# Local and global attention, then a gated feed-forward: four word and four merged buffers for the weight conversion, and the short product of the global queries issued first

## The chip, the cores and the metric

The kernel runs on one core of a Trainium2 chip. A core has five engines that run their own instruction queues and meet at semaphores: TensorE (matrix products; PE in the profile, with its weight loads as PEld), VectorE (DVE), ScalarE (ACT), GpSimd (POOL) and SyncE (SP), which here only issues transfers. The metric is the time of one execution on the device, in microseconds (us); lower is better.

## The reference: what is computed

Eight batches of eight heads, 512 local positions with 64 dimensions, and 32 global tokens. A local query sees the local keys within 32 positions and all global keys; a global query sees all keys. The attention output, 4608 rows of 512, goes through a gated feed-forward layer of width 1536.

```python
k_all, v_all = concat(k_g, k_l), concat(v_g, v_l)
out_g = softmax(q_g @ k_all.T / 8) @ v_all
s_ll  = where(abs(i - j) <= 32, q_l @ k_l.T / 8, -1e9)
out_l = softmax(concat(q_l @ k_g.T / 8, s_ll)) @ concat(v_g, v_l)
x     = concat(out_g, out_l) as rows of 8 heads * 64
y     = (sigmoid(x @ w_gate) * (x @ w_val)) @ w_out
```

The three weight matrices reach the device as 64-bit floating-point numbers: `w_gate` and `w_val` 512 x 1536, `w_out` 1536 x 512.

## The kernel before

**Precision by two terms.** A float32 operand is split into a rounded part (`hi`) and the remainder (`lo`), both of a type that TensorE takes in one pass; a product is then three products, hi*hi, lo*hi and hi*lo. Where a tile is called native (`nat`), float32 is multiplied as it is, without a split. That is so in the first two chunks and in the first four heads of the third.

**Chunks.** The rows are worked in chunks: two of 256 rows for batch 0, then one of 512 rows for each other batch, and at the end one of 256 rows that holds the global tokens of all batches. For each chunk `ffn_stream` yields the products of the feed-forward layer piece by piece: for each of 12 blocks of the inner width (`f`), twelve products for the gate (`bank_g`, L380), twelve for the value (`bank_v`, L380), then those with `w_out` (`bank_o`, L414). The attention of a later chunk runs between them.

**An order by due times.** `att_events` gives each step of the attention a due time, counted in pieces of the feed-forward stream; L496 to L518 put these steps and the weight conversion into one list, sort it by time and order number, and L520 to L526 run the steps as the stream reaches their times. Steps due at or before zero run ahead of the stream. What the code issues is then laid out, engine by engine, by the scheduler of the programming layer, which also gives out the slots of the tile pools and sets the semaphores.

**Attention units.** A head of a full chunk has two local units (`local_unit`) and one global unit (`global_unit`). A local unit: scores into `bank_x` (L237), mask and row minimum on VectorE (L251), exponential on ScalarE (L254), scaling (L223 or L225), transposes through TensorE into `bank_y` (L268), a copy to `pt` (L276 native; else L279 for the rounded part and L280 for the remainder), products with the values (L290 and L291 native, L298 and L299 split). A global unit: the 32 global queries of the head, `qg`, against all keys. The four windows of local keys go in two halves into `sa`, a `bank_x` tile of 32 x 512 (L317); the 32 global keys go into `sb`, a `bank_y` tile of 32 x 32 (L319). Each needs two products in the split case, so that the unit has four with 256 columns and two with 32, all with `qg` as the stationary operand. Then the maxima of both (L322, L323), the exponentials (L326, L327), scaling, transposes (L335) and the products with the values (L348). All of `bank_x`, `bank_y`, `bank_g` and `bank_v` share four banks of PSUM (tag `att`). In the units of the first chunk TensorE also runs `fill`, small products whose result nothing uses (L113).

**Weight conversion.** The weights are fetched as words, two 32-bit words a number, in 36 pieces: for each `f`, 128 columns of `w_gate`, the same of `w_val`, and 128 rows of `w_out` (`w_src`). `stage(i)` has SP load piece i, 512 KB, into a word buffer (L129). `convert(i, hi, lo)` builds float32 from the words in a merged buffer: the sign (L140), the high word rescaled on VectorE or ScalarE by turns (L146 or L144), the low word's bits (L147), the high word's bits (L148); ScalarE rounds that into `hi` (L149), GpSimd subtracts for `lo` (L150). At its end it calls `stage` for the next piece that takes the same word buffer. Pieces 0 to 2 are tied by `issue_after` to the last L251 issued at that point; later pieces are not. The converted `w_gate` and `w_val` stay in SBUF; `w_out` goes to device memory (L161, L162) and is fetched again for each use (L405).

**Buffers.** One tile of the pool `xp`, `words`, of 4096 words a partition, holds three word buffers of 1024 and two merged buffers of 512 (L476 to L478). Piece i takes buffer i modulo their number. The pool has two slots; the other holds `xts[0]`, the input of the feed-forward layer for the first two chunks. L513 starts the loads of the first three pieces at the time -1002. The operands `q` and `k` of the first chunk's heads are loaded at -1016 (heads 0 and 1), -1008 (2 and 3), -1000 (4 and 5) and -992 (6 and 7), the values at -1004 and -988.

Of the kernel before, what the change touches and what calls it, by code (L numbers as in the profile page):

```python
# [10 lines left out]
U32 = mybir.dt.uint32  # L11
# [6 lines left out]
P = 128  # L18
# [38 lines left out]
def kernel(ctx, tc, qk, v, w_gate, w_val, w_out, out_l, out_g):  # L57
    nc = tc.nc
# [4 lines left out]
    const = ctx.enter_context(tc.tile_pool(name="const", bufs=1))  # L63
# [52 lines left out]
    conv_bufs = []  # L116
# [8 lines left out]
    def stage(i):  # L125
        if i < len(w_src):
            src = w_src[i]
            st = conv_bufs[0][i % len(conv_bufs[0])].rearrange("p (t n) -> p t n", t=src.shape[1])
            nc.sync.dma_start(st, src)  # L129
# [91 lines left out]
    def scaled(kind, out, in_, by):  # L221
        if NORM[kind][cnt["norm"] % len(NORM[kind])] == "s":
            nc.scalar.mul(out, in_, by)  # L223
        else:
            nc.vector.tensor_scalar(out, in_, by, None, op0=ALU.mult)  # L225
        cnt["norm"] += 1
# [78 lines left out]
    def global_unit(T, b, h):  # L305
        ks, k0s, q0 = T["qk"], T["k0"], T["q0"]
        nat = T["native"]
        last = len(ks) - 1
        prow, kt = 64 * (h % 2), h // 2
        qg = ks[0][:, QK - SG - q0:QK - q0]  # L310
        sa = ps.tile([32, 4, P], F32, name="bank_x", tag="att", bufs=4)
        sb = ps.tile([32, 32], F32, name="bank_y", tag="att", bufs=4)
        for half in range(2):
            o0 = 96 * half
            for t, (src, k0) in enumerate(zip(ks, k0s)):
                view = src[:, k0 + 32:k0 + 32 + 4 * BLK].rearrange("p (j c) -> p j c", c=BLK)[:, :, o0:o0 + 64]
                nc.tensor.matmul(sa[:, :, 64 * half:64 * half + 64], qg, view, start=t == 0, stop=t == last)  # L317
        for t, (src, k0) in enumerate(zip(ks, k0s)):
            nc.tensor.matmul(sb, qg, src[:, k0 + 96:k0 + 128], start=t == 0, stop=t == last)  # L319
        mg = small.tile([32, 4], F32, name="mg")  # L320
        saf = sa.rearrange("p a c -> p (a c)")
        nc.vector.tensor_reduce(mg[:, 0:1], saf, axis=AX.X, op=ALU.max)  # L322
        nc.vector.tensor_reduce(mg[:, 1:2], sb, axis=AX.X, op=ALU.max)  # L323
        nc.vector.tensor_scalar(mg[:, 2:3], mg[:, 0:1], mg[:, 1:2], -0.125, op0=ALU.max, op1=ALU.mult)
        sg = small.tile([32, 2], F32, name="sg")
        nc.scalar.activation(pg[:, 0:512], saf, AF.Exp, bias=mg[:, 2:3], scale=0.125, accum_out=sg[:, 0:1])  # L326
        nc.scalar.activation(pg[:, 544:576], sb, AF.Exp, bias=mg[:, 2:3], scale=0.125, accum_out=sg[:, 1:2])  # L327
        yield
        nc.vector.tensor_scalar(mg[:, 3:4], sg[:, 0:1], sg[:, 1:2], 1e-9, op0=ALU.add, op1=ALU.add)
        nc.vector.reciprocal(mg[:, 3:4], mg[:, 3:4])  # L330
        scaled(0, pg[:, 0:576], pg[:, 0:576], mg[:, 3:4])
        yield
        pt_ps = ps.tile([P, 5, 32], F32, name="bank_y", tag="att", bufs=4)
        for j in range(5):
            nc.tensor.transpose(pt_ps[:, j], pg[:, j * P:(j + 1) * P], ident[0:32, 0:32])  # L335
        if nat:
            pt = att.tile([P, 5, 32], F32, name="ptg_nat", tag="ptg", bufs=1)
            nc.scalar.copy(pt, pt_ps)
        else:
            pt = att.tile([P, 5, 64], F32R, name="ptg", bufs=1)  # L340
            nc.scalar.copy(pt[:, :, 0:32], pt_ps)
            nc.vector.tensor_tensor(pt[:, :, 32:64], pt_ps, pt[:, :, 0:32].bitcast(F32), op=ALU.subtract)
        yield
        vt = T["v"]
        xg = xg32[prow:prow + 64, kt, b * SG:(b + 1) * SG]
        o_ps = ps.tile([64, 32] if nat else [P, 64], F32, name="bank_x", tag="att", bufs=4)
        for j in range(5):
            nc.tensor.matmul(o_ps, vt[:, (VM + VS)[j], :], pt[:, j, :], start=j == 0, stop=j == 4)  # L348
        if nat:
            nc.scalar.copy(xg, o_ps)  # L350
            return
        y = att.tile([64, 64], F32, name="y", bufs=1)
        nc.scalar.copy(y, o_ps[64:128])
        nc.vector.tensor_tensor(y, o_ps[0:64], y, op=ALU.add)
        nc.gpsimd.tensor_tensor(xg, y[:, 0:32], y[:, 32:64], op=ALU.add)
# [118 lines left out]
    xts = {0: xp.tile([P, 2, KT, 512], F32R, name="xt")}  # L474
    xts[1] = xts[0]
    words = xp.tile([P, 4096], U32, name="xt")  # L476
    conv_bufs.append([words[:, i * 1024:(i + 1) * 1024] for i in range(3)])
    conv_bufs.append([words[:, 3072 + i * 512:3072 + (i + 1) * 512] for i in range(2)])  # L478

    chs = []  # L480
    for ci, (b, blocks, _) in enumerate(chunks):
# [14 lines left out]
    queue = att_events(0, -1000, START["per0"]) + att_events(1, START["base1"], START["per1"])  # L496
# [10 lines left out]
    for f in range(NF):  # L507
# [2 lines left out]
        queue.append((g, 4, lambda f=f: convert_w(f, 0)))  # L510
        queue.append((v_, 4, lambda f=f: convert_w(f, 1)))
        queue.append((o, 4, lambda f=f: convert_wo(f)))
    queue.append((-1002, 2, lambda: [stage(i) for i in range(3)]))  # L513

    def split_globals():
        for kt in range(KT):
# [65 lines left out]
```

## Time and profile before

| | us |
|---|---|
| three runs, median | 1262.37 |
| their lowest and highest | 1262.34, 1264.86 |
| the profiled execution | 1262.67 |
| its span, first to last instruction | 1260.8 |
| ScalarE: L254 busy | 113.8 |
| GpSimd: L401 busy | 137.6 |
| VectorE: L225 into `p_buf` busy | 151.8 |

How to read the lines further down: a group of instructions gives line, engine, operation, tiles (out<-in), shapes and count; after the bar the busy time and the mean duration of one in ns; after the second bar the engine's idle time just before them, and what ended it. A line of the timeline gives the start and the duration in us, then engine, line and operation; a count above one means merged neighbours, and the bracket at its end tells the idle time before it and the releaser. A stretch gives for each engine the busy time and, in brackets, the number of instructions.

### The profile page before, as it was taken

How to read it: one execution, taken by the hardware profiler on the slowest of the kernel's cores; microseconds unless marked ns; L12 is line 12 of the kernel's file. 1: busy time of each engine (PE TensorE's matmuls, PEld its weight loads, DVE VectorE, ACT ScalarE, POOL GpSimd, SP SyncE). 2: the span in 40 equal slices, each digit the busy share in tenths (PEclk: the TensorE clock that was granted, in tenths of full speed). 3: DMA queues.
4: the chain of work that ended last, by engine and by line, in shares of the span. 5: the costliest groups of instructions: out<-in, count | busy, mean ns of one | idle time of the engine just before them, and what ended most of it. 6: DMA issues, size and time to landing. Idle time of an engine off the chain costs nothing.

```text
span 1260.8 us, 20601 instructions
## 1 busy us (share of the span) xinstructions
PE 1223.5 (97%) x6884; PEld 998.6 (79%) x6884; DVE 878.9 (70%) x2433; ACT 782.9 (62%) x1899; POOL 571.1 (45%) x573
## 2 busy tenths in 40 slices
PE   8899989999999999999999999999999999999998
PEld 6677768788778877888788877888788877888897
DVE  6888977757876778758776778767875787632232
ACT  5686766756666666656765766656665666532333
POOL 2444545535555455545554455535554545311111
PEclk9798999999999999999999999999999999999999
DMA  6686754333333333333334333333333332122243
GB/s 232 215 264 219 255 172 125 107 97 108 92 103 113 113 92 108 109 106 112 100 86 120 121 100 100 108 112 109 91 107 114 108 92 88 51 84 67 67 134 117
DMA packets 59497, 151.90 MB, mean 120 GB/s; under 512 B 6144, under 2 KB 19456, under 8 KB 59392
## 3 DMA queue, kind: packets, MB, share of 16 engines
q1 hardware_dynamic: 59392, 150.59, 39.3%
q8 instruction: 54, 0.88, 0.3%
q14 instruction: 51, 0.42, 0.1%
HBM read 135.36 MB, written 15.20 MB: 119 GB/s over the span
## 4 chain that ended last, share of the span: by engine, by line
PE 73%; DVE 16%; ACT 6%; issue 4%; DMA 1%; POOL 0%; POOLq 0%; DVEq 0%; ACTq 0%; SPq 0%
PE bank_g L380 19%; PE bank_v L380 18%; PE bank_o L414 18%; PE bank_x L237 4%; PE bank_y L268 4%; DVE p_buf L225 3%; DVE th L396 2%; PE bank_y L335 2%; PE bank_x L348 2%; DVE pg_buf L225 2%; PE bank_x L298 2%; ACT s_sb L254 1%; PE bank_x L299 1%; PE bank_x L317 1%; DVE pt L280 1%
## 5 line engine op out<-in xcount | busy, mean ns | idle before, releaser
L380 PE MATMUL bank_g<-xt,wg 128*128 128x512 f32 (+1 forms) x1440 | 340.2, 371 | 1.8 <-DVE th L398 1.8
L380 PE MATMUL bank_v<-xt,wv 128*128 128x512 f32 (+1 forms) x1440 | 332.7, 368 | 3.0 <-DVE pt L280 2.7
L414 PE MATMUL bank_o<-wo,hh 128*128 128x512 f32 x1224 | 334.1, 404 | 0.8 <-ACT hh L400 0.4
L380 PEld LDWEIGHTS bank_g<-xt,wg 128*128 128x128 f32 x1440 | 238.6, 191 | 41.7 <-issue 3.5
L380 PEld LDWEIGHTS bank_v<-xt,wv 128*128 128x128 f32 x1440 | 237.8, 190 | 40.7 <-PE bank_y L319 3.1
L414 PEld LDWEIGHTS bank_o<-wo,hh 128*128 128x128 f32 x1224 | 214.1, 189 | 38.9 <-ACT hh L400 1.2
L401 POOL TENSOR_TENSOR hh<-th,hh 128x512 fp32r<-128x512 f32 (+1 forms) x120 | 137.6, 1147 | 200.7 <-ACT hh L400 199.8
L254 ACT ACTIVATE s_sb<-s_sb,nm 128x224 f32<-128x224 f32 x240 | 113.8, 475 | 142.9 <-DVE nm L251 141.8
L225 DVE TENSOR_SCALAR p_buf<-s_sb,r 128x128 f32<-128x128 f32 (+1 forms) x443 | 151.8, 386 | 4.2 <-PE bank_y L268 0.4
L393 DVE TENSOR_SCALAR mn<-bank_g 128x512 f32<-128x512 f32 (+1 forms) x108 | 67.3, 623 | 110.8 <-ACT th L388 109.4
L396 DVE SCALAR_TENSOR_TENSOR th<-th,mn 128x512 f32<-128x512 f32 (+1 forms) x120 | 102.0, 850 | 59.9 <-ACT mn L394 53.6
L206 POOL TENSOR_TENSOR kl<-qk_raw,qk_hi 128x704 fp32r<-128x704 f32 x52 | 88.4, 1700 | 116.0 <-ACT qk_hi L205 116.0
L303 POOL TENSOR_TENSOR x<-t 64x256 f32<-64x256 f32 x104 | 76.1, 732 | 142.7 <-DVE t L302 138.5
L388 ACT ACTIVATE th<-bank_g 128x512 f32<-128x512 f32 (+1 forms) x120 | 63.5, 530 | 98.0 <-PE bank_g L380 96.5
L400 ACT CAST hh<-th 128x512 fp32r<-128x512 f32 (+1 forms) x120 | 66.5, 554 | 68.6 <-DVE th L398 68.1
L251 DVE CUSTOM_DVE_ANT_0 s_sb<-bank_x,masks 128x224 f32<-128x224 f32 x240 | 83.8, 381 | 12.6 <-PE bank_x L237 8.2
L208 POOL TENSOR_TENSOR qk_hi<-qk_raw,qk_hi 64x256 fp32r<-64x256 f32 x104 | 87.8, 863 | 4.1
L268 PE MATMUL bank_y<-ident,p_buf 128*128 128x128 f32 x496 | 78.7, 279 | 9.4 <-DVE p_buf L225 5.1
L268 PEld LDWEIGHTS bank_y<-ident,p_buf 128*128 128x128 f32 x496 | 60.3, 142 | 29.5 <-ACT pg_buf L326 6.6
L257 DVE TENSOR_SCALAR r<-sm 128x2 f32<-128x2 f32 x128 | 29.3, 229 | 75.8 <-ACT s_sb L254 74.1
L205 ACT CAST qk_hi<-qk_raw 128x1248 fp32r<-128x1248 f32 x52 | 64.1, 1233 | 22.3 <-PE bank_y L319 22.2
L398 DVE TENSOR_TENSOR th<-bank_v,th 128x512 f32<-128x512 f32 (+1 forms) x120 | 72.4, 603 | 5.0 <-PE bank_v L380 1.3
(111 smaller groups left out, 1994.6 us busy)
## 6 DMA issues: line engine op xcount, KB each, us to landing
wo<-wo_dram SPq DMA_DIRECT2D x116, 512.0 KB, 3.5
qk_raw<-in_qk_dram SPq DMA_DIRECT2D x104, 312.0 KB, 4.5
v_raw<-in_v_dram SPq DMA_DIRECT2D x52, 256.0 KB, 2.6
out_dram<-ob SPq DMA_DIRECT2D x34, 256.0 KB, 2.9
xt<-in_w_gate_dram SPq DMA_DIRECT2D x12, 512.0 KB, 4.7
xt<-in_w_val_dram SPq DMA_DIRECT2D x12, 512.0 KB, 4.1
xt<-in_w_out_dram SPq DMA_DIRECT2D x12, 512.0 KB, 4.9
v_nat<-in_v_dram SPq DMA_DIRECT2D x8, 512.0 KB, 4.5
```

What stands on the lines that cost most here:

```text
L206: nc.gpsimd.tensor_tensor(kl, t[:, K0:Q1], hi[:, K0:Q1].bitcast(F32), op=ALU.subtract)
L208: nc.gpsimd.tensor_tensor(hi[64:128, r], t[64:128, r], hi[64:128, r].bitcast(F32), op=ALU.subtract)
L225: nc.vector.tensor_scalar(out, in_, by, None, op0=ALU.mult)
L251: anchor[0] = nc.vector.tensor_tensor_reduce(out=s_sb[:, i], in0=s_ps[:, i, 0:WIN], in1=masks[:, m], scale=-0.125, scalar=3.0e38, op0=ALU. ...
L254: nc.scalar.activation(s_sb[:, i], s_sb[:, i], AF.Exp, bias=nm[:, i:i + 1], scale=-1.0, accum_out=sm[:, i:i + 1])
L268: nc.tensor.transpose(pt_ps[:, 2 * i + t], pb[:, i, t * P:(t + 1) * P], ident)
L303: nc.gpsimd.tensor_tensor(dst, t0[:, :, 0], t0[:, :, 1], op=ALU.add)
L380: nc.tensor.matmul(acc, w[a][:, t, fs], xt[:, c, t, x0:x0 + ntok], start=n == 0, stop=n == 11)
L396: nc.vector.scalar_tensor_tensor(th, th, 1.0, mn, op0=ALU.add, op1=ALU.mult)
L398: nc.vector.tensor_tensor(th, acc, th, op=ALU.mult)
L401: nc.gpsimd.tensor_tensor(hh[:, 1, 0:ntok], th, hh[:, 0, 0:ntok].bitcast(F32), op=ALU.subtract)
L414: nc.tensor.matmul(o_ps[t], ph[:, a, t * P:(t + 1) * P], pwo[:, c], start=f2 == 0 and i == 0, stop=f2 == NF - 1 and i == 2)
```

## The change

1. In `global_unit` the two products into `sb` are issued ahead of the four into `sa`. The tiles are still allocated in the same order.
2. A new tile `more` of 2048 words a partition gives a fourth word buffer and, together with the end of `words`, four merged buffers in place of two.
3. The loads of four pieces, not three, are started at the time -1002. `convert` takes the number of buffers from the lists, so that it now stages the piece four further on.
4. The scratch for DMA descriptors in SBUF is set to 1024.

```diff
         sb = ps.tile([32, 32], F32, name="bank_y", tag="att", bufs=4)
+        for t, (src, k0) in enumerate(zip(ks, k0s)):
+            nc.tensor.matmul(sb, qg, src[:, k0 + 96:k0 + 128], start=t == 0, stop=t == last)
         for half in range(2):
...
                 nc.tensor.matmul(sa[:, :, 64 * half:64 * half + 64], qg, view, start=t == 0, stop=t == last)
-        for t, (src, k0) in enumerate(zip(ks, k0s)):
-            nc.tensor.matmul(sb, qg, src[:, k0 + 96:k0 + 128], start=t == 0, stop=t == last)
...
-    conv_bufs.append([words[:, i * 1024:(i + 1) * 1024] for i in range(3)])
-    conv_bufs.append([words[:, 3072 + i * 512:3072 + (i + 1) * 512] for i in range(2)])
+    more = const.tile([P, 2048], U32, name="words_more")
+    room = [words[:, i * 512:(i + 1) * 512] for i in range(8)] + [more[:, i * 512:(i + 1) * 512] for i in range(2048 // 512)]
+    conv_bufs.append([words[:, i * 1024:(i + 1) * 1024] for i in range(3)] + [more[:, i * 1024:(i + 1) * 1024] for i in range(1)])
+    conv_bufs.append((room[6:8] + room[8 + 2 * 1:])[0:4])
...
-    queue.append((-1002, 2, lambda: [stage(i) for i in range(3)]))
+    queue.append((-1002, 2, lambda: [stage(i) for i in range(4)]))
...
-    nc = bacc.Bacc("TRN2", target_bir_lowering=False, num_devices=1)
+    nc = bacc.Bacc("TRN2", target_bir_lowering=False, num_devices=1, dynamic_dma_scratch_size=1024)
```

## The prediction

> **What bounds the kernel now.** The page first: the totals, the strip of forty slices, the chain that ended last.
>
> ```profile
> span 1260.8 us, 20601 instructions
> PE 1223.5 (97%) x6884; PEld 998.6 (79%) x6884; DVE 878.9 (70%) x2433; ACT 782.9 (62%) x1899; POOL 571.1 (45%) x573
> ...
> PEclk9798999999999999999999999999999999999999
> ...
> PE 73%; DVE 16%; ACT 6%; issue 4%; DMA 1%; POOL 0%; POOLq 0%; DVEq 0%; ACTq 0%; SPq 0%
> ```
>
> TensorE is busy 97% of the span and carries 73% of the chain; VectorE is next with 16%. The strip says where to look closer: the granted clock falls below full only in the first slices. The view by stretches splits the span (columns: PE, PEld, DVE, ACT, POOL busy, then clock, DMA share, GB/s).
>
> ```profile
> 4.00:12.00 8.00, 8.00 (x52) 7.24 (x53) 3.76 (x20) 1.97 (x8) 0.00 (x0) 1.00 1.03 361
> 36.00:50.00 14.00, 12.65 (x49) 10.06 (x50) 8.74 (x26) 7.44 (x18) 5.96 (x5) 0.53 0.72 238
> 97.00:100.40 3.40, 2.19 (x18) 1.51 (x17) 3.40 (x9) 1.58 (x5) 1.62 (x2) 1.00 0.82 284
> 100.40:107.20 6.80, 6.80 (x24) 4.83 (x25) 5.66 (x18) 3.57 (x13) 0.55 (x1) 0.50 0.69 241
> 110.70:114.10 3.40, 3.40 (x17) 3.18 (x16) 2.75 (x8) 2.42 (x7) 0.29 (x1) 0.50 0.14 52
> 115.00:172.00 57.00, 50.32 (x330) 39.16 (x329) 55.22 (x126) 39.15 (x111) 29.76 (x23) 1.00 0.77 245
> 172.10:175.50 3.40, 3.40 (x17) 3.40 (x17) 1.42 (x7) 2.87 (x10) 2.33 (x3) 0.50 0.28 101
> 260.00:360.00 100.00, 99.08 (x546) 80.99 (x545) 74.32 (x209) 63.85 (x153) 47.51 (x49) 1.00 0.34 104
> ```
>
> There are two regimes. From about 220 us on TensorE sets the pace (99.08 of 100 us busy). Before about 175 us the weights are converted between the attention units, and the pace changes hands: VectorE holds it from 115 to 172 (55.22 of 57 us), TensorE at about half clock from 36 to 50 and in three shorter stretches. The first part of the change acts in both regimes, the buffers in the early one only.
>
> **Part 1: the short product first.** A global unit issues four long products (L317, 256 columns) and two short ones (L319, 32 columns). One unit from the timeline (columns: start, duration, engine, line):
>
> ```profile
> 328.12 0.18 PE L319 MATMUL bank_y<-kl,qk_hi 128*32 128x32 f32 x1
> 328.16 1.19 PE L414 MATMUL bank_o<-wo,hh 128*128 128x512 f32 x4
> ...
> 329.87 0.36 PE L298 MATMUL bank_x<-pt,vhl 128*128 128x256 f32 x1 [0.52 <-DVE pt L280]
> ...
> 330.30 0.28 PE L299 MATMUL bank_x<-pt,vhl 128*128 128x256 f32 x1
> 330.42 1.09 PE L414 MATMUL bank_o<-wo,hh 128*128 128x512 f32 x4
> ```
>
> Four products of L414 take 1.19 us behind the short product and 1.09 us behind a 256-column one. I read the 0.10 us as a weight load that the short product is too short to cover. The load rows give a second measure:
>
> ```profile
> L299 PEld LDWEIGHTS bank_x<-pt,vhl 128*128 128x128 f32 x208 | 39.2, 188 | 2.4
> L317 PEld LDWEIGHTS bank_x<-kl,qk_hi 128*32 128x32 f32 x104 | 11.2, 108 | 6.7
> L319 PE MATMUL bank_y<-kl,qk_hi 128*32 128x32 f32 x52 | 9.5, 183 | 0.0
> L319 PE MATMUL bank_y<-qk_nat 64*32 64x32 f32 x24 | 2.7, 192 | 0.0
>   PEld bank_v L380: 3.1, 6
> ```
>
> A 128-column load takes 188 ns, a 32-column load 108: 80 ns less. With the short products first, what stands uncovered behind them is the 32-column load of the first long product, and the 128-column load of whatever follows the unit lies under the last long one. So 0.08 to 0.10 us a unit; I take 0.08. There are 52 such units (L319 x52, one of each kind a unit): 52 x 0.08 = 4.2 us gross. Not all reaches the end. In 6 units TensorE waits about 0.5 us right behind L319 anyway (the last row, from the view of L319: who waited for it). In units like the one shown, TensorE meets a wait for VectorE's L280 four products later, and gets there earlier for nothing; I count 6 of these, one for each waiting unit, since the pattern repeats with the chunk. That leaves 40 x 0.08 = **-3.2 us**, bounds -4.2 and 0. The 12 units of the early heads (L319 x24, two a unit) lie where VectorE often sets the pace: 12 x 0.08 = 1.0, half of it kept, **-0.5 us** (0 to -1.2). The long product is ready two short ones later for the reduction L322; one short product follows the other within 0.02 to 0.04 us above, and L322 stood in its queue until 330.24 in that unit, so I cost this at nothing; uncovered it would be 64 x 0.06 = 3.8 us at most.
>
> [...]
>
> **Part 2: four merged buffers.** L140 writes a merged buffer that POOL's L150 of two pieces earlier must have read.
>
> ```profile
> L140 DVE TENSOR_SCALAR xt<-xt 128x512 uint32<-128x512 uint32 x36 | 22.1, 615 | 4.7 <-POOL wg L150 2.3 <-POOL wo_lo L150 1.2 <-POOL wv L150 1.2
> L147 DVE SCALAR_TENSOR_TENSOR xt<-xt 128x512 uint32<-128x512 uint32 x36 | 26.4, 734 | 0.0
> L148 DVE SCALAR_TENSOR_TENSOR xt<-xt 128x512 uint32<-128x512 uint32 x36 | 29.1, 808 | 0.7 <-DVE p_buf L225 0.3 <-ACT xt L144 0.2
> ...
> 39.81 0.43 DVE L140 TENSOR_SCALAR xt<-xt 128x512 uint32<-128x512 uint32 x1 [1.16 <-POOL wg L150]
> 43.47 0.43 DVE L140 TENSOR_SCALAR xt<-xt 128x512 uint32<-128x512 uint32 x1 [1.16 <-POOL wv L150]
> 45.78 0.39 DVE L251 CUSTOM_DVE_ANT_0 s_sb<-bank_x,masks 128x224 f32<-128x224 f32 x1 [1.43 <-PE bank_x L237]
> ...
> 92.91 0.43 DVE L140 TENSOR_SCALAR xt<-xt 128x512 uint32<-128x512 uint32 x1 [1.17 <-POOL wg L150]
> ...
> 152.61 0.43 DVE L140 TENSOR_SCALAR xt<-xt 128x512 uint32<-128x512 uint32 x1 [1.18 <-POOL wo_lo L150]
> ```
>
> Four waits, 4.7 us in all. The first two lie in the half-clock stretch, and VectorE waits 1.43 us for TensorE right after: worth nothing. The third precedes the TensorE gap at 97 to 100, the fourth lies where VectorE is busy 55.22 of 57 us: 1.17 + 1.18 = **-2.3 us** (0 to -4.7).
>
> **Part 3: four word buffers.** No wait of VectorE for a load of words appears in these rows, so the depth itself removes nothing. What moves is the start: SP now issues a fourth load of 512 KB ahead of the operands of heads 4 and 5.
>
> ```profile
> q1 hardware_dynamic: 59392, 150.59, 39.3%
> ...
> qk_nat<-in_qk_dram SPq DMA_DIRECT2D x1, 320.0 KB, 8.0
> ...
> 3.76 0.93 SPq L174 DMA_DIRECT2D qk_nat<-in_qk_dram  x2
> ...
> 11.83 0.64 PE L237 MATMUL bank_x<-qk_nat 64*128 64x224 f32 x2
> ```
>
> Issued at 3.76, landed 8.0 us later at about 11.8, used at 11.83: no slack. At the 361 GB/s of 4 to 12 us, 524 KB take 1.45 us: **+1.4 us** (0 if another transfer gives way, +1.5 at most), and the start is a serial chain that carries it on.
>
> The fourth piece's words also no longer wait for the first piece's, so its conversion can start much earlier. The queue is not in program order even now:
>
> ```profile
> 32.47 1.43 DVE L140 TENSOR_SCALAR xt<-xt 128x512 uint32<-128x512 uint32 x1
> 33.89 0.41 DVE L140 TENSOR_SCALAR xt<-xt 128x512 uint32<-128x512 uint32 x1
> 34.30 0.67 DVE L147 SCALAR_TENSOR_TENSOR xt<-xt 128x512 uint32<-128x512 uint32 x1
> 34.88 1.26 DVE L225 TENSOR_SCALAR p_buf<-s_first,r 128x128 f32<-128x128 f32 x4
> 35.31 0.52 PE L268 MATMUL bank_y<-ident,p_buf 128*128 128x128 f32 x2 [3.00 <-DVE p_buf L225]
> ```
>
> One piece's L140 stands ahead of the previous piece's L147: a planner places each instruction by when its operands come free. Here the conversions hold back L225, and TensorE waits 3.00 us. A piece costs VectorE 615 + 734 + 808 ns = 2.2 us. If the fourth piece moves into VectorE's idle time before 17 us, up to 2.2 us of that wait go; if it lands in front of a softmax step, 2.2 us are added. I take **-1.0 us**, nearer to the gain, because VectorE was busy 3.76 of the 8 us in the first row. The smaller scratch for DMA descriptors costs nothing: the kernel's 150.59 MB move on the hardware queue, which the first of the rows on the start shows, and no data on any other.
>
> **Sum** against the profiled execution (1262.67 us, span 1260.8, 1.9 us around it): -3.2 - 0.5 - 2.3 + 1.4 - 1.0 = -5.6, so 1257.1. The median of the runs is 0.3 lower, so **1257 us**.
>
> **The rivals.**
>
> 1. *Conversions jump the softmax queue: slower.* Place: VectorE's queue from 12 to 36 us. The late load costs 1.4, the fourth piece falls before softmax steps (+2.2), another is drawn ahead of L225 at 34.88 (+2.2), and the longer TensorE gap stretches the half-clock stretch by 6.8 us (+3.4, taken at half rate). With -3.7 of Part 1: +5.5, 1268. It decides if L225 falls more than about 3.7 us later. For it: the rows of 32 to 35 show exactly this already. Against: VectorE's idle time in the first 12 us. 16%.
> 2. *The gain sits behind VectorE: no change.* Part 1's lead is taken by later waits for L280 and L225 (1.0 left), only one POOL wait counts (-1.2), the load costs 1.4: -0.8, 1261.5. For it: VectorE is 74% busy even in the steady regime. Against: TensorE's 99%. 19%.
> [...]
> 4. *The half-clock stretches after 100 us vanish.* They follow stretches in which TensorE idled (2.19 of 3.40 busy). Three of them last 6.8 + 3.4 + 3.4 = 13.6 us; at full clock TensorE's work there takes 6.8 us less, of which I keep 5 since VectorE is busy too: 1252. 15%.
>
> [...]
>
> **How the numbers follow.** Forecast 46% (1254 to 1259.8); the rivals 16, 19, 4 and 15%. About 0.2% (2.5 us) is what a measurement of this kernel can tell from no change. Faster: 46 + 15 = 0.61; same: 19 + 4 = 0.23; slower: 0.16. The low ends -4.2 - 1.2 - 4.7 - 2.2 add to about 1250, rival 4 gives 1252: low 1251. The high ends without Part 1 are +1.5 + 2.2: 1266; high 1265, which leaves out most of rival 1 and a little of rival 4.
>
> **What would show it.** [...] Part 2: L140's row without its 4.7 us. Part 3: L237 of heads 4 and 5 at about 13.2 instead of 11.83; the wait before L268 near 35 us shorter than 3.00 or, for rival 1, longer. The clock strip decides rival 4. The forecast is wrong if the planner orders the steady units anew: a single extra wait of 0.5 us a chunk would cost as much as Part 1 brings.

## The result and the profile after

The changed kernel is slower: 1271.61 us (median of four, 1270.28 to 1273.43) against 1263.36 us for the kernel before beside it on the same chip (1262.34 to 1264.86), a ratio of 1.0067 [1.0053, 1.0081]. The forecast was 1257 us, the range 1251 to 1265: wrong in sign, and outside the range. The profiled execution, the highest of the four, took 1273.43 us, with these lines of its page:

```profile
span 1271.6 us, 20613 instructions
PE 1227.6 (97%) x6884; PEld 994.9 (78%) x6884; DVE 872.4 (69%) x2433; ACT 781.9 (61%) x1899; POOL 575.9 (45%) x573
...
PEclk9797989999999999999999999999999999999999
...
PE 71%; DVE 14%; ACT 6%; issue 4%; POOL 1%; DMA 1%; POOLq 0%; DVEq 0%; ACTq 0%
```

Totals hardly say anything: TensorE is busy 4.1 us longer, VectorE 6.5 us less, and GpSimd's share of the chain goes from 0 to 1%. The clock strip differs in the fourth and the sixth slice, that is between 95 and 191 us. Three stretches of the kernel before, then the same of the changed one (columns: stretch, length, busy time of PE, PEld, DVE, ACT, POOL, then the granted clock, DMA share, GB/s):

```profile
20.00:200.00 180.00, 165.00 (x1039) 128.31 (x1038) 150.84 (x409) 125.37 (x366) 83.61 (x67) 0.92 0.68 214
110.00:125.00 15.00, 14.01 (x91) 11.98 (x90) 14.03 (x30) 9.17 (x26) 7.71 (x7) 0.89 0.57 184
200.00:1250.00 1050.00, 1036.27 (x5717) 852.57 (x5717) 716.11 (x1976) 646.02 (x1505) 483.41 (x491) 1.00 0.34 102
```

```profile
20.00:200.00 180.00, 159.82 (x955) 119.90 (x955) 139.81 (x392) 117.61 (x347) 81.96 (x61) 0.89 0.63 206
110.00:125.00 15.00, 9.28 (x67) 6.66 (x67) 10.04 (x24) 7.38 (x21) 9.61 (x5) 0.84 0.59 201
200.00:1250.00 1050.00, 1035.92 (x5730) 848.27 (x5730) 716.82 (x1989) 648.89 (x1514) 487.72 (x494) 1.00 0.34 102
```

Behind 200 us TensorE is as busy as it was: 1036 us of 1050 in both. That the loss is complete by then is shown by the stores of the third chunk's output, before and after; the changed kernel is 10.4 us late there and 10.8 at its end:

```profile
413.78 4.68 SPq L423 DMA_DIRECT2D out_dram<-ob  x4
```

```profile
424.19 4.67 SPq L423 DMA_DIRECT2D out_dram<-ob  x4
```

So the loss lies in the conversion stage, and two terms of the first rows account for it. **TensorE's waits**: 180 - 165.00 = 15.0 us before, 20.2 after, +5.2. **Half clock**: the clock's records of both profiles hold only 1.00 and 0.50, so that a mean clock of 0.92 is 0.08 x 2 x 180 = 28.8 us at half speed, 0.89 is 39.6. In the changed kernel four products of L237 take 1.02 us at 1.00 (from 94.65) and 1.86 at 0.50 (from 103.85); so I estimate that the 10.8 us more cost half of it where TensorE works throughout, +5.4. Together 10.6, and the span grew by 10.8. The closeness is in part luck, since two digits of clock leave up to 1.8 us open: by the clock's own records half clock lasts 27.3 us before and 41.0 after, +13.7, of which half is 6.8.

The largest single piece stands in the second rows: from 110 to 125 us VectorE, TensorE and ScalarE do less, and only GpSimd is busy longer. The timeline there (start, duration, engine, line), VectorE's middle rows left out:

```profile
116.72 5.69 POOL L150 TENSOR_TENSOR wg<-xt,wg 128x512 fp32r<-128x512 f32 x1 [3.59 <-ACT wg L149]
116.77 0.50 DVE L225 TENSOR_SCALAR pg_buf<-pg_buf,mg 32x576 f32<-32x576 f32 x1
117.19 0.67 DVE L147 SCALAR_TENSOR_TENSOR words_more<-xt,words_more 128x512 uint32<-128x512 uint32 x1
117.80 0.41 DVE L140 TENSOR_SCALAR words_more<-words_more 128x512 uint32<-128x512 uint32 x1
...
120.61 0.67 DVE L147 SCALAR_TENSOR_TENSOR xt<-xt 128x512 uint32<-128x512 uint32 x1
122.37 0.72 POOL L401 TENSOR_TENSOR hh<-th,hh 128x256 fp32r<-128x256 f32 x1
123.14 1.22 PE L414 MATMUL bank_o<-wo,hh 128*128 128x512 f32 x2 [4.93 <-POOL hh L401]
```

GpSimd's subtraction L150, usually 1.3 to 1.5 us, takes 5.69. Meanwhile VectorE runs nine instructions without a gap, eight of them from three conversion pieces by turns; the last ends at 121.28, and L150 ends 1.13 us after that, as though it had only then begun. L401 of the feed-forward stream stands behind it in GpSimd's queue, and TensorE waits 4.93 us for L401. It happens once more at 166.99 (6.02 us). L401 and the next L150 stand behind it in GpSimd's queue, ScalarE waits for that L150, and only then reaches its L350 (176.92), for which TensorE waits 3.58 us, until 177.15:

```profile
174.95 0.62 ACT L362 CAST xt<-x 128x512 fp32r<-128x512 f32 x1 [4.63 <-POOL wg L150]
```

Such lengths are new. The view of L150, first before (of its three groups the one with the longest), then after (columns: shortest/median/longest in ns):

```profile
L150 POOL TENSOR_TENSOR wv<-xt,wv x12: 1272/1512/2493, 29.2 to 169.3; 128x512 fp32r<-128x512 f32 x12
```

```profile
L150 POOL TENSOR_TENSOR wg<-xt,wg x6: 1253/1389/5690, 23.1 to 173.7; 128x512 fp32r<-128x512 f32 x6
...
L150 POOL TENSOR_TENSOR wo_lo<-xt,wo_hi x6: 1264/1276/6019, 44.0 to 167.0; 128x512 fp32r<-128x512 f32 x6
```

Half clock comes here with TensorE's waits: it sets in at 99.76 behind one of 1.19 us (for L225, until 98.77), at 120.24 during the 4.93 us for L401, and at 178.26 behind the 3.58 us for L350. Not every wait brings it: behind one of 1.26 us until 15.14 the clock stays at 1.00. These three stretches of the changed kernel, cut just inside the clock's records, answer to the three that the prediction shows for the kernel before (from 100.4, 110.7 and 172.1 us); each is longer, by 3.4, 6.8 and 3.4 us:

```profile
99.76:110.00 10.24, 10.24 (x40) 7.47 (x39) 5.83 (x19) 5.63 (x18) 2.79 (x2) 0.50 0.67 232
...
120.24:130.40 10.16, 7.26 (x31) 6.24 (x32) 1.47 (x4) 2.57 (x7) 4.80 (x4) 0.50 0.28 106
...
178.26:185.00 6.74, 6.74 (x23) 4.19 (x23) 3.63 (x12) 4.29 (x14) 3.07 (x3) 0.50 0.62 194
```

### The profile page after: what moved, and what is told of

It is laid out like the page before. It is cut to its first block, busy times and chain, and to the rows that moved or that the text cites. A ratio compares the mean times of both kernels' runs of the same rounds, so it can differ in the third digit from the quotient of the medians.

```text
span 1271.6 us, 20613 instructions
## 1 busy us (share of the span) xinstructions
PE 1227.6 (97%) x6884; PEld 994.9 (78%) x6884; DVE 872.4 (69%) x2433; ACT 781.9 (61%) x1899; POOL 575.9 (45%) x573
## 4 chain that ended last, share of the span: by engine, by line
PE 71%; DVE 14%; ACT 6%; issue 4%; POOL 1%; DMA 1%; POOLq 0%; DVEq 0%; ACTq 0%
PE bank_g L380 19%; PE bank_o L414 18%; PE bank_v L380 17%; PE bank_x L237 4%; PE bank_y L268 3%; DVE p_buf L225 3%; DVE th L396 2%; PE bank_x L348 2%; PE bank_y L335 2%; ACT s_sb L254 2%; PE bank_x L298 2%; PE bank_x L319 2%; PE bank_x L299 1%; DVE pg_buf L225 1%; DVE pt L280 1%
## 5 line engine op out<-in xcount | busy, mean ns | idle before, releaser
L380 PE MATMUL bank_g<-xt,wg 128*128 128x512 f32 (+1 forms) x1440 | 339.2, 370 | 0.0
L380 PE MATMUL bank_v<-xt,wv 128*128 128x512 f32 (+1 forms) x1440 | 330.5, 367 | 2.6 <-DVE mg L323 2.6
L380 PEld LDWEIGHTS bank_g<-xt,wg 128*128 128x128 f32 x1440 | 239.3, 192 | 39.6 <-issue 4.2
L380 PEld LDWEIGHTS bank_v<-xt,wv 128*128 128x128 f32 x1440 | 236.6, 189 | 42.3 <-PE bank_x L319 4.2
L401 POOL TENSOR_TENSOR hh<-th,hh 128x512 fp32r<-128x512 f32 (+1 forms) x120 | 137.2, 1144 | 194.0 <-ACT hh L400 193.4
L225 DVE TENSOR_SCALAR p_buf<-s_sb,r 128x128 f32<-128x128 f32 (+1 forms) x443 | 149.0, 379 | 4.5 <-PE bank_y L268 0.6
L251 DVE CUSTOM_DVE_ANT_0 s_sb<-bank_x,masks 128x224 f32<-128x224 f32 x240 | 83.5, 382 | 19.9 <-PE bank_x L237 10.6
L268 PE MATMUL bank_y<-ident,p_buf 128*128 128x128 f32 x496 | 77.1, 277 | 12.0 <-ACT xg L350 3.8
L268 PEld LDWEIGHTS bank_y<-ident,p_buf 128*128 128x128 f32 x496 | 60.4, 141 | 31.4 <-ACT pg_buf L326 6.8
```

Of the source, the lines that this page charges most:

```text
L251: anchor[0] = nc.vector.tensor_tensor_reduce(out=s_sb[:, i], in0=s_ps[:, i, 0:WIN], in1=masks[:, m], scale=-0.125, scalar=3.0e38, op0=ALU. ...
L268: nc.tensor.transpose(pt_ps[:, 2 * i + t], pb[:, i, t * P:(t + 1) * P], ident)
L380: nc.tensor.matmul(acc, w[a][:, t, fs], xt[:, c, t, x0:x0 + ntok], start=n == 0, stop=n == 11)
L401: nc.gpsimd.tensor_tensor(hh[:, 1, 0:ntok], th, hh[:, 0, 0:ntok].bitcast(F32), op=ALU.subtract)
```

## The experiments

Three theories were set against each other. **S**: with four merged buffers VectorE no longer has to wait for GpSimd, runs conversions back to back, and GpSimd's subtractions stand meanwhile. **W**: the fourth word buffer and its early load. **O**: the order into which the scheduler puts the queues once the short product comes first.

### Parts of the change alone

e1, the order without the buffers; e2, the buffers without the order; e3, four merged and three word buffers; e4, four word and two merged buffers. e1's edit is the first part of the change's diff, e2 the rest of it. e3 and e4 also have the tile `more` and the smaller descriptor scratch, and e4 starts four loads. The buffers of e3, then of e4:

```diff
+    conv_bufs.append([words[:, i * 1024:(i + 1) * 1024] for i in range(3)])
+    conv_bufs.append(room[6:10])
```

```diff
+    conv_bufs.append([words[:, i * 1024:(i + 1) * 1024] for i in range(3)] + [more[:, 0:1024]])
+    conv_bufs.append([words[:, 3072 + i * 512:3072 + (i + 1) * 512] for i in range(2)])
```

> Only the short product is issued first; the buffers are as before. Theory S (the loss comes from VectorE's conversions running back to back once four merged buffers let them, while GpSimd's L150 stands still and the products behind it wait): ratio 0.998 to 1.001, no L150 over 2.6 us; the steady part gains at most 1 us, since the 0.08 us a unit is taken back by waits for L280. Theory W (the loss comes from the fourth word buffer and its early load): the same here. Theory O (the loss comes from the new order of the queues that the short product brings): ratio 1.004 or more.

> Four word and four merged buffers, the products of the global unit in the old order. Theory S and theory W: ratio 1.005 to 1.009, and S asks for at least one L150 of 4 us or more with a TensorE wait of 3 us or more behind it. Theory O: ratio within 0.002 of 1.

> Three word buffers as before, four merged buffers, old order of the products. Theory S: ratio 1.003 or more, with at least one L150 of 4 us or more, since nothing holds L140 to GpSimd's pace; the waits of L140 for L150 are gone. Theory W: faster than before by the 2.3 us of the two waits, ratio 0.997 to 0.999.

> Four word buffers with the fourth load at the start, two merged buffers as before, old order of the products. Theory S: no L150 over 2.6 us, ratio within 0.002 of 1. Theory W: ratio 1.005 or more, with the loss before 120 us.

Measured: e1 1.0033 [1.0020, 1.0047], e2 1.0043 [1.0027, 1.0059], e3 1.0046 [1.0031, 1.0061], e4 1.0011 [0.9999, 1.0022]. W falls. The order and the buffers each cost; e1 and e2 add to 1.0076, and the change has 1.0067. Neither S nor O holds as stated: e1 costs where S allowed 1.001 at most, and e2 costs where O allowed 1.002. S's sign stands in e2, one L150 of 6.01 us and a wait of TensorE of 3.57 us behind it, for a smaller loss than S asked:

```profile
159.93 6.01 POOL L150 TENSOR_TENSOR wo_lo<-xt,wo_hi 128x512 fp32r<-128x512 f32 x1 [2.47 <-ACT wo_hi L149]
...
170.08 0.66 PE L268 MATMUL bank_y<-ident,p_buf 128*128 128x128 f32 x4 [3.57 <-ACT xg L350]
```

In e3 the sign is missing: no L150 is long (2.56 us at most, where S asked for 4). But L401 itself is (3.83 us at most), with TensorE behind it:

```profile
114.22 3.11 POOL L401 TENSOR_TENSOR hh<-th,hh 128x256 fp32r<-128x256 f32 x1 [2.15 <-ACT hh L400]
...
117.38 0.79 PE L414 MATMUL bank_o<-wo,hh 128*128 128x512 f32 x1 [2.46 <-POOL hh L401]
```

L401 of this size takes 0.72 us elsewhere. e8 has three merged buffers, as a dose between two and four:

```diff
+    conv_bufs.append([words[:, 3072:3584], words[:, 3584:4096], more[:, 0:512]])
```

> Three merged buffers, three word buffers, old order. Theory S: VectorE may run one piece further ahead than before and one less than with four, so the loss is smaller than the 0.46% of four: ratio 1.000 to 1.004, with the longest L150 or L401 between 2 and 4 us. Rival (the removed waits are worth their 2.3 us and something else costs in the four-buffer kernel): 0.997 to 0.999.

Measured 1.0016 [1.0006, 1.0027], with an L150 of 3.41 and an L401 of 3.83 us: two, three and four merged buffers give 0, +0.16 and +0.46%.

### Where the order costs

e6 has the short product first in the 52 split units only, e7 in the 12 native ones only. Diff of e6 (e7 has the two conditions exchanged):

```diff
+        if not nat:
+            for t, (src, k0) in enumerate(zip(ks, k0s)):
+                nc.tensor.matmul(sb, qg, src[:, k0 + 96:k0 + 128], start=t == 0, stop=t == last)
         for half in range(2):
...
+        if nat:
+            for t, (src, k0) in enumerate(zip(ks, k0s)):
+                nc.tensor.matmul(sb, qg, src[:, k0 + 96:k0 + 128], start=t == 0, stop=t == last)
```

> The short product is issued first in the 52 split units alone; the 12 native units of the early heads and the buffers are as before. Theory: each unit's 0.08 us is taken back at the next L298, which waits for VectorE's L280 in either order, and what made the order alone slower lies in the early native units: ratio 0.999 to 1.001. Rival: the order itself costs in the steady part: 1.002 or more.

> The short product first in the 12 native units alone. Theory: these move the order of the queues in the conversion stage, and the cost of the order is here: ratio 1.002 to 1.004. Rival: the cost lies in the split units, within 0.001 of 1.

Measured: e6 0.9996 [0.9983, 1.0008], e7 1.0033 [1.0020, 1.0046]. The 52 units to which Part 1 gave -3.2 us are worth nothing that can be told from zero; the whole cost of e1 comes from 12 units that lie in the conversion stage (50 to 188 us in the kernel before). The unit shown in the prediction, in the changed kernel, where L319 is now the long product:

```profile
338.26 0.28 PE L319 MATMUL bank_x<-kl,qk_hi 128*32 128x256 f32 x1
338.38 1.09 PE L414 MATMUL bank_o<-wo,hh 128*128 128x512 f32 x4
340.43 0.36 PE L298 MATMUL bank_x<-pt,vhl 128*128 128x256 f32 x1 [0.97 <-DVE pt L280]
```

The four products behind it take 1.09 us, 0.10 less, as Part 1 has it; but the wait for L280 grows from 0.52 to 0.97 us and takes the lead back.

### VectorE against GpSimd, by itself

Five kernels ask what lets VectorE shut GpSimd out. They hold nothing but rows of VectorE instructions beside one GpSimd subtraction of L150's size. e5 and e9 (contiguous operands; one tile, then two by turns):

```diff
+            for j, o in enumerate(ops):
+                v = vs[0 if o == "s" else j % 2]
...
+                    nc.vector.scalar_tensor_tensor(v, s1u, 29, v, op0=ALU.logical_shift_right, op1=ALU.bitwise_or)
...
+            nc.gpsimd.tensor_tensor(lo, s2, hi.bitcast(F32), op=ALU.subtract)
```

> The disputed cost by itself: nothing of the reference is computed (the outputs are zeros). A GpSimd subtraction of 128x512 is started a little after a row of VectorE instructions of one kind: none, 2, 4 or 8 two-input shifts as in L147, 8 one-input ANDs as in L140, 8 multiplications as in L146, 8 products that read PSUM, and 8 that alternate between the L147 form and the PSUM form. Theory S: GpSimd makes no progress until the row ends, so its instruction takes about 1.3 us alone and grows with the row, by about 0.6 us for each further two-input instruction: about 2, 3 and 5.5 us for 2, 4 and 8; with the alternating row it gets in at the first gap, under 3 us. A lock that is handed over after each instruction gives at most one VectorE instruction of delay, 2 us whatever the row.

> Nothing of the reference is computed (the outputs are zeros). The GpSimd subtraction is started beside a row of VectorE instructions that do not depend on their predecessor, since they write two tiles by turns, as they do where the planner mixes two pieces: 2, 4 and 8 two-input shifts, 8 as in the conversion (shift, AND, shift, multiplication), 8 that read PSUM, 8 that alternate shift and PSUM; and, as before, 8 on one tile. Theory S in its new form (GpSimd is shut out only while each VectorE instruction starts before its predecessor has ended, which dependent ones do not): 1.3 us alone and on one tile, over 4 us beside 8 by turns, growing with the row. If the independence does not matter: 1.3 us in all.

The subtraction took 1.26 to 1.31 us in e5, and one VectorE instruction of the row was stretched instead, by up to 1.1 us (0.69 to 1.78), except in the row whose instructions all read PSUM (0.69 each); in e9 it took 1.72 us at most:

```profile
70.47 5.97 DVE L95 SCALAR_TENSOR_TENSOR v_two<-s,v_two 128x512 uint32<-128x512 uint32 x8 [0.74 <-ACT s L89]
71.16 1.72 POOL L102 TENSOR_TENSOR lo_two<-s,hi 128x512 fp32r<-128x512 f32 x1 [2.58 <-ACT s L90]
```

So in these rows the delay was one instruction at most, on either side (that a lock does it is not shown), and S seemed to fall. But only one row of the two kernels mixed the forms of the conversion (e9, 1.31 to 1.45 us), and the subtraction always began 0.4 to 0.7 us into its row. e13 has the row of the stall as it stood (three pieces in turn, every second word, L225 at the head), e14 sweeps the subtraction's start over rows of L147 alone, and e15 compares rows of one form with rows that mix the 0.41 us single-operand form (L140, L146) with L147:

```diff
+            for j in range(13):
+                w, v = big[j % 3], vs[j % 3]
...
+                o = ops[j % len(ops)] if 0 < j < 12 else "L"
+                if o == "A":
+                    nc.vector.tensor_scalar(v, high, 0x80000000, None, op0=ALU.bitwise_and)
...
+                elif o == "L":
+                    nc.vector.scalar_tensor_tensor(v, low, 29, v, op0=ALU.logical_shift_right, op1=ALU.bitwise_or)
```

> Nothing of the reference is computed: rows of VectorE instructions in the forms of the conversion stage run beside one GpSimd subtraction of 128x512, three times each. Between the two kinds of rows measured before (at most 1.72 us) and the changed kernel (5.69 us) stand the strided operands of L140, L146, L147 and L148 (every second word), three pieces in turn, and L225 on 32 partitions at the head. Rows: rowS, the row of the stall at 116.77 us (L225, then three pieces in turn, strided); rowC, the same with operands that lie together; row2, a row twice as long; rowE, the subtraction's operand ready before the row; mixS, L147 alone on three pieces; oneS, one piece; nog, without L225. Theory S (VectorE shuts GpSimd out by the form of the row): the subtraction takes 4 to 6 us beside rowS and rowE, 8 to 11 beside row2 if it lasts to the row's end, and 1.3 to 1.8 beside rowC if the stride does it. Rival (something else of the kernel holds GpSimd's subtraction, and the row is only what ran beside it): 1.2 to 2 us beside every row.

> Nothing of the reference is computed: 36 rows of twelve VectorE instructions in the form of L147 (0.605 us apart in the run before), each beside one GpSimd subtraction of 128x512, which becomes ready at nine points from about 0.9 to 1.3 us after the row's start (over half of the spacing of the row's instructions). Nine rows each on one tile with operands that lie together, one tile strided, three tiles in turn together, three in turn strided. In the run before, subtractions stood 7 to 14 us beside some rows and 1.26 us beside others. Phase theory: what decides is the moment at which the subtraction becomes ready; each kind of row has some of about 1.3 us and some of 6 to 7.5 us, which end 1.26 us after the row's last instruction. Stride theory: 6 to 7.5 us beside all strided rows, 1.3 to 1.9 us beside all others. Independence theory: 6 to 7.5 us beside all rows of three tiles, 1.3 to 1.9 us beside one tile.

> Nothing of the reference is computed: 48 rows of thirteen VectorE instructions by turns on three tiles, each beside one GpSimd subtraction that becomes ready at six moments (over 0.4 us). The forms: L147 alone, L147 by turns with L140, L147 by turns with L146, and all four of L140, L146, L147, L148; each with strided operands (every second word) and with operands that lie together. The runs before: beside rows of L147 alone the subtraction never took more than 1.83 us, strided or not; beside mixed rows it stood 7 to 14 us. Mixture theory: 5 to 8 us in some of the rows that mix the single-operand form (L140, L146; 0.41 us) with L147, whatever the stride. Mixture and stride: the same in the strided mixed rows alone. Neither, if all rows give 1.3 to 1.9 us: then another part of the rows measured before (the 32-partition L225 at the head, their length) is needed.

e13 has it. One of its two longest subtractions (14.15 and 14.16 us), and the last VectorE instruction beside it:

```profile
80.05 14.15 POOL L124 TENSOR_TENSOR lo_oneS<-s,hi 128x512 fp32r<-128x512 f32 x1 [2.56 <-ACT s L104]
...
92.40 0.67 DVE L121 SCALAR_TENSOR_TENSOR v<-words,v 128x512 uint32<-128x512 uint32 x1
```

VectorE had fallen behind there and ran several rows without a gap, so that the row beside a subtraction is not always the one that it is named after; the subtraction ends at 94.20, 1.13 us behind VectorE's last instruction (93.07), the same 1.13 us as in the changed kernel. Seven of the 21 subtractions stood 7.2 to 14.2 us, the other fourteen took 1.26 to 1.31. In e14 none of 36 took more than 1.83 us, whatever the start, the stride and the number of tiles: for rows of L147 alone all three theories of its expectation fall. In e15 none of 12 beside L147 alone took more than 1.82, but 14 of 36 beside mixed rows stood 4.97 to 6.78, strided or not:

```profile
53.33 1.82 POOL L113 TENSOR_TENSOR lo_LLstr<-s,hi 128x512 fp32r<-128x512 f32 x1 [7.67 <-ACT s L95]
...
126.38 6.78 POOL L113 TENSOR_TENSOR lo_LAstr<-s,hi 128x512 fp32r<-128x512 f32 x1 [7.34 <-ACT s L95]
...
389.37 6.33 POOL L113 TENSOR_TENSOR lo_LHAMtog<-s,hi 128x512 fp32r<-128x512 f32 x1 [5.99 <-ACT s L95]
```

That GpSimd can be shut out until VectorE's row ends is shown by itself (14.15 us in e13), and mixing the forms was enough for it at some moments of the start (14 of 36 in e15).

### Does taking it away mend the kernel?

First by order: e10 to e12 tie each conversion, from the fourth piece on, behind the previous piece's L148, so that pieces do not mix on VectorE; e10 on e3, e11 on the changed kernel, e12 on the kernel before.

```diff
-        with tc.issue_after(anchor[0].ins) if i < 3 else nullcontext():
+        with tc.issue_after((anchor[0] if i < 3 else chain[0]).ins):
...
-            nc.vector.scalar_tensor_tensor(v, high, 3, v, op0=ALU.logical_shift_left, op1=ALU.bitwise_or)
+            chain[0] = nc.vector.scalar_tensor_tensor(v, high, 3, v, op0=ALU.logical_shift_left, op1=ALU.bitwise_or)
```

> Four merged and three word buffers as in the kernel with merged buffers alone, old order of the products, but VectorE's instructions of one piece are issued only behind the last one of the piece before, so that no two pieces are mixed on its queue. Theory S: the successive instructions of a piece depend on each other and let GpSimd in; no L150 or L401 over 2.6 us, and the ratio falls from 1.0046 to 1.002 or below. If the loss comes from the run-ahead as such or from the memory layout: the ratio stays at 1.003 or more.

> The changed kernel with the same issue order of the pieces. Theory S: the two L150 of 5.7 and 6.0 us are gone, the ratio falls from 1.0067 by at least 0.003, to the cost of the native units' order, 1.001 to 1.004. Otherwise 1.005 or more.

> The kernel before with the same issue order of the pieces, buffers and products unchanged: what the issue order does by itself. With two merged buffers VectorE waits for GpSimd anyway; ratio within 0.002 of 1, longest L150 no longer than before (2.5 us).

Measured: e10 1.0059 [1.0044, 1.0074], e11 1.0027 [1.0012, 1.0042], e12 1.0090 [1.0075, 1.0104]. e11 came out as S said: the longest L150 is 1.83 us and the changed kernel is 0.4% faster than without the tie. e10 did not: S asked for 1.002 or less and no L150 over 2.6 us, and one of 3.06 is left. And the tie alone costs the kernel before 0.9% (longest L150 2.88 us), where 0.2% at most was expected. With it the whole change gains 0.6% (1.0027 against 1.0090) and four merged buffers 0.3%. So the sign of the change depends on how VectorE's queue happens to be laid out.

Then by form: e16 (on the changed kernel), e17 (on the kernel before) and e18 (on the changed kernel, with the order of e6) take the single-operand form out of the conversions.

```diff
-REBASE = "vs"
+REBASE = "s"
...
-            nc.vector.tensor_scalar(v, high, 0x80000000, None, op0=ALU.bitwise_and)
+            nc.vector.scalar_tensor_tensor(v, high, 0x80000000, high, op0=ALU.bitwise_and, op1=ALU.bitwise_and)
```

> The changed kernel with VectorE's single-operand forms taken out of the conversions: L140 masks with two tensor operands (0.67 us in place of 0.41), L146 goes to ScalarE for every piece (0.68 us of L144 there). VectorE's work changes by 36 x 0.26 - 18 x 0.41 = +2.0 us, ScalarE's by 18 x 0.68 = +12 us, of which TensorE should see little. The outputs are the same. Theory M (a row of VectorE that mixes the 0.41 and the 0.67 us forms shuts GpSimd out until its first gap; rows of one form let it in after one instruction): no L150 over 2.5 us, and 1260 to 1268 us. Rival Q (the order of the queues, with or without long subtractions): 1268 to 1278 us, with or without them. If L150 still stands over 4 us, M falls.

> The kernel before with the same two edits: what they cost by themselves. Theory M: L150 stays under 2.5 us as it is, so nothing but the added work can show: 1262 to 1268 us. The change is then worth e16 against e17: 0 to 4 us faster by M (the units it moves were worth nothing, the buffers free the L140 that waited 4.7 us), slower still by 3 us or more by Q.

> As e16, with the short product first only in the 52 split units (the native ones cost 4.8 us by themselves in e7). M and the earlier runs together: 2 to 5 us under e16, 1258 to 1264 us, the only combination that could come out below the kernel before. Q: no nearer to it than e2, 1266 to 1270 us.

Measured: e16 1.0089 [1.0074, 1.0104], e17 1.0074 [1.0057, 1.0091], e18 1.0061 [1.0044, 1.0078] (1273.44, 1271.25 and 1269.74 us). All three lie above M's ranges, and e16 and e18 in Q's; e16 is 2.2 us slower than e17, between M's forecast and Q's. M also falls by its own condition: e16 still has an L150 of 4.18 us (and an L401 of 4.10), e18 one of 4.68. The one of e16 stands beside a row of the two-operand form alone, headed by an L225 that ends 0.04 us after the subtraction has begun.

```profile
124.28 0.67 DVE L147 SCALAR_TENSOR_TENSOR words_more<-words_more 128x512 uint32<-128x512 uint32 x1
124.32 4.18 POOL L150 TENSOR_TENSOR wv<-words_more,wv 128x512 fp32r<-128x512 f32 x1 [0.28 <-ACT wv L149]
124.89 0.67 DVE L140 SCALAR_TENSOR_TENSOR xt<-xt 128x512 uint32<-128x512 uint32 x1
125.49 0.67 DVE L148 SCALAR_TENSOR_TENSOR words_more<-words_more 128x512 uint32<-128x512 uint32 x1
126.09 0.67 DVE L147 SCALAR_TENSOR_TENSOR xt<-xt 128x512 uint32<-128x512 uint32 x1
126.69 0.67 DVE L140 SCALAR_TENSOR_TENSOR xt<-xt 128x512 uint32<-128x512 uint32 x1
```

So the mixture is enough in e15, and in the kernel a row without it does the same (4.18 us), unless the L225 at its head counts; what exactly lets GpSimd in stays open. And e17, whose longest L150 is 2.41 us, lost 0.74% all the same: being shut out is not the only way to lose time in this stage.

### One account for all of them

The two terms of the first section, from the same row (20 to 200 us) of each kernel's view by stretches, against the kernel before: TensorE's busy time, the clock, the added waits plus half of the added half-clock time, how late the first store of the third chunk is issued (413.78 us in the kernel before), and the difference of the measured span.

| kernel | PE busy | clock | waits + half clock | third chunk | span |
|---|---|---|---|---|---|
| before | 165.00 | 0.92 | | | 1260.8 |
| e4 words | 163.51 | 0.93 | 1.5 - 1.8 = -0.3 | +0.1 | +1.7 |
| e6 order, split | 166.04 | 0.91 | -1.0 + 1.8 = 0.8 | +1.0 | +1.7 |
| e8 three merged | 162.12 | 0.91 | 2.9 + 1.8 = 4.7 | +3.5 | +4.1 |
| e1 order | 163.08 | 0.92 | 1.9 + 0 = 1.9 | +2.9 | +3.9 |
| e7 order, native | 163.15 | 0.91 | 1.9 + 1.8 = 3.7 | +3.6 | +4.3 |
| e2 buffers | 160.73 | 0.93 | 4.3 - 1.8 = 2.5 | +3.4 | +4.4 |
| e3 merged | 162.89 | 0.91 | 2.1 + 1.8 = 3.9 | +2.2 | +5.3 |
| e18 split, forms | 164.14 | 0.89 | 0.9 + 5.4 = 6.3 | +5.5 | +6.7 |
| e11 change, tied | 162.85 | 0.89 | 2.2 + 5.4 = 7.6 | +7.3 | +8.5 |
| e17 before, forms | 162.51 | 0.89 | 2.5 + 5.4 = 7.9 | +7.3 | +10.7 |
| after | 159.82 | 0.89 | 5.2 + 5.4 = 10.6 | +10.4 | +10.8 |
| e16 change, forms | 165.04 | 0.86 | 0.0 + 10.8 = 10.8 | +10.2 | +11.1 |
| e10 merged, tied | 158.72 | 0.90 | 6.3 + 3.6 = 9.9 | +10.7 | +13.2 |
| e12 before, tied | 159.35 | 0.87 | 5.7 + 9.0 = 14.7 | +13.4 | +16.5 |

Two of these rows as they stand in the view, of e16 and of e12:

```profile
20.00:200.00 180.00, 165.04 (x950) 122.41 (x951) 150.67 (x373) 126.71 (x362) 84.45 (x61) 0.86 0.62 203
```

```profile
20.00:200.00 180.00, 159.35 (x932) 122.78 (x932) 148.13 (x384) 116.57 (x340) 76.97 (x61) 0.87 0.65 206
```

The account meets the third chunk within 1.7 us in every kernel, about what two digits of clock leave open, and the span within 3.3, mostly from below. What is missing there comes behind 414 us, where the account does not look: up to 3.4 us, 3.1 of the 5.3 in e3, 1.6 of the 1.7 in e4, 0.4 in the changed kernel. In e3 TensorE's waits for L280 behind 460 us are 6.3 us in all against 3.7 before; the other kernels were not followed there. In e16 TensorE is busy as long as before and gets 89 fewer products done: its loss is clock alone.

The rows are of one profiled execution each, and the clock's part is not the same in every execution of one program. The kernel before, in its executions on record, runs from 1258.31 us at a mean clock of 0.992 to 1266.34 at 0.986. Of ten executions of e11, six had 0.989 to 0.991 and took 1263.98 to 1268.62 us, four had 0.983 or 0.984 and took 1270.80 to 1271.91; the row is one of these four. The rows of e10, e12 and e17 too are their longest executions, 2 to 5 us over the medians. The changed kernel's four all have 0.983 to 0.987.

## Why the prediction was wrong

**The step that failed is Part 2, "Four waits ... -2.3 (0 to -4.7)".** The waits did go. The view of L140 in the changed kernel has a single wait, for the fourth load, whose piece VectorE now converts first, at 13.45 us:

```profile
its engine sat idle before it (us, times) until:
  DMA words_more<-in_w_gate_dram: 4.7, 1
```

But the bounds excluded a loss, since the term counted VectorE's time and asked nothing of the engine it had waited for. The wait for L150 was also the gap in which GpSimd ran. Four merged buffers alone cost 0.46% (e3), some +5.8 us at 1263, where -2.3 was forecast; up to the third chunk of its profile, and so in the stage that the term was about, the cost is +2.2. How much of that is the shutting out, and how much another order of the queues, the runs do not separate: e11 without long subtractions is 0.4% better than the changed kernel, but e17 and e12, whose longest L150 are 2.41 and 2.88 us, lose as much without them.

**Part 1, -3.2 for the split units:** the gain was there, 0.10 us in the unit shown (that an uncovered load is its cause was an estimate of the author's and is not shown), and worth next to nothing at the end (e6: -0.5 us, between -2.1 and +1.0). The step "I count 6 of these, one for each waiting unit" failed. The view of L298 in the kernel before, narrowed to the weight loads, would have said so (columns: releaser, us, times):

```profile
its engine sat idle before it (us, times) until:
  DVE pt L280: 14.7, 33
```

L298 runs in 104 local units (208 loads, two a unit), and 33 loads already waited for VectorE, 14.7 us in all; TensorE's 99% there was no proof that it sets the pace, since a lead of 0.1 us only has to reach the next such wait. That is rival 2's mechanism. **-0.5 for the native units:** measured +0.33% (e7), about +4.2 us. There the moved product changes the order of the queues around it; the bounds 0 to -1.2 excluded that too. This is the second step that failed, and it cost nearly as much as Part 2.

**Part 3, +1.4 and -1.0:** e4 gives +0.11% with an interval that holds zero; the forecast of +0.4 us lies in it. But the +1.4 rested on a wrong reading. "Issued at 3.76, landed 8.0 us later at about 11.8, used at 11.83: no slack" joins a load to a product that does not read it: in the changed kernel that load is issued at 4.93 and lands 9.4 us later, at about 14.3, and the same L237 runs at 11.55.

```profile
qk_nat<-in_qk_dram SPq DMA_DIRECT2D x1, 320.0 KB, 9.4
...
11.55 0.64 PE L237 MATMUL bank_x<-qk_nat 64*128 64x224 f32 x2
...
15.14 0.43 PE L290 MATMUL bank_x<-pt_nat,v_nat 128*64 128x128 f32 x2 [1.26 <-ACT pt_nat L276]
```

In both traces this L237 waits for the semaphore of the second load, issued at 1.19 before and at 1.18 after, so it ran 0.3 us earlier, not at 13.2; TensorE waits 1.26 us a little later. The -1.0 came in part: the fourth piece goes first, and the wait before L268 near 35 us is 2.28 instead of 3.00. That the first product of L380 starts at 43.43 instead of 42.95, near the sum of +0.4, is luck for a sum with one wrong term. e4 does not test the -1.0, since with two merged buffers its first L140 runs at 17.66, no earlier than before.

**The rivals.** Rival 1, slower at 1268, came nearest, but not in its place (VectorE's queue from 12 to 36 us): the loss lies from about 100 us on, and its sign, a longer wait near 35 us, is not there; its 6.8 us more half clock behind that wait is not shown either, the stretch there lasts 13.65 us in both profiles. Rival 4 had the right quantity and the wrong sign: the half-clock stretches behind 99 us grew from 13.65 to 27.31 us in all. Rival 3, the 4% among the chances, said that the order of the products is worth nothing; it falls, since the order did move them by 0.10 us. The half-clock stretches were the warning in the profile: a stage whose clock drops behind some of its waits can answer to a new wait with more than its price: in the changed kernel 5.2 us of waits came with 5.4 us of clock (6.8 by its records).

## What to carry to other kernels

A wait of one engine for another is not only a cost: before it is taken away, ask what the other engine does in that gap, and give the term an upper end. In a stage where two engines are nearly full and the clock drops behind some gaps, count TensorE's waits and its half-clock time over the whole stage, and do not book a removed wait as a gain before the queues are laid out anew: of the fourteen kernels of this case that differ from the one before, twelve are slower than it beyond their intervals and none is faster. A lead won on the busiest engine was worth nothing here (e6, 0.9996) where the next wait for another engine stood a few products behind it.

## What the runs showed of the hardware

GpSimd's subtraction of 128x512 can stand through a whole row of VectorE instructions, 14.15 us instead of 1.26 in e13, and ends some 1.13 us behind the row's last instruction, as though it began only there. In the rows of e5 and e9 the delay is one instruction at most, on either side (1.72 us for the subtraction, 1.78 instead of 0.69 for a VectorE instruction), and there is none for the row of e5 whose instructions all read PSUM (0.69 each, the subtraction 1.26 to 1.27). e13, e15 and the changed kernel go beyond that, since there the subtraction stands as though GpSimd got no turn between the instructions of a row (up to 14.16, 6.78 and 6.02 us). What holds it up is not shown; the runs show only which rows do it.

The other surprise is the size of the clock's part: e12, with nothing changed but the order in which VectorE gets the conversions, has 18 us more at half clock in its profile (a mean of 0.87 against 0.92 over 180 us; one stretch at 0.50 lasts 20.48 us, from 159.29 to 179.77), and is the slowest of all. Between 20 and 200 us the stretches at half clock last 13.65, 6.83, 3.41 and 3.41 us in the kernel before and 13.65, 10.24, 10.24 and 6.83 us in the changed one, all of them, like the 20.48 us of e12, whole multiples of 3.41 us.
